# The second MoE's w_in products by Strassen's scheme, in spans of 768 tokens

## The chip, the cores and the metric

The kernel runs on one core of a Trainium2 chip. The metric is the device time of one execution in microseconds. The core's engines are TensorE (matmuls into PSUM), VectorE, ScalarE, GpSimd and SyncE, which issues all DMAs of this kernel; each works off its own instructions in the written order.

## What is computed

Retention attention over 8 batches, 8 heads, 576 positions and 64 dimensions, then two MoE layers over the 4608 tokens of width 512:

```python
x = attn_out.transpose(0, 2, 1, 3).reshape(4608, 512)
x = np.maximum(np.maximum(x @ w1, x @ w2), x @ w3) @ w_out   # first MoE, d_ff 768
h = x @ w_in                                                 # second MoE, d_ff 2048
g = h * np.clip(h + 3.0, 0.0, 6.0) / 6.0
out = g @ w_out
```

The weights come in as 64-bit floats and are turned into 32-bit ones on the chip. Every operand of a large matmul is split into a rounded high part and the rest (fp32r), and a product of two is three matmuls: high by high, high by rest, rest by high (`product`, L378).

## The kernel before, in words

The tokens are worked in nine blocks of 512 (TT = 9, TB = 512). Attention of block t + 1 is mixed into the first MoE of block t. `up` (L388) makes one product of the first MoE, 4 k-tiles by 3 matmuls of 512 columns; its result is copied by ScalarE (L397) or joined by VectorE (L399) and then split (`split`, L50: ScalarE rounds, VectorE subtracts). `down` (L404) sums the six hidden blocks into four PSUM tiles `o0` to `o3`; at the last one the four parts are split into `y` and stored to DRAM as `x2d`, high part and rest. Beside this, one step of `background` after every fourth block unpacks the second MoE's 32 weight tiles (`Weights.step`: VectorE, ScalarE and GpSimd) and stores them as `wbd`. In the last two token blocks they are read back into SBUF, where they then stay.

The second MoE loops over nine token blocks and, inside, 16 hidden blocks of 128 (the loop behind `drain`, L609). `hidden` (L560) is 12 matmuls of 512 columns: the weights are the stationary operand, the tokens stream. `gated` (L567) has VectorE form min(max(h + 3, 0), 6) h in two operations out of PSUM (L570, L571), ScalarE round it (L52), VectorE subtract (L53). `project` (L577) is 12 matmuls of 512 columns as well: the gated hidden block is stationary, w_out streams, and four 128-token rows of the output gather in `o0` to `o3` over all 16 hidden blocks. It runs two hidden blocks behind, so the gating has cover. `store` (L593) scales the four tiles (L600 VectorE, L603 ScalarE) into one of three `ob` tiles and issues their DMAs (L605). The next token block's `x` is loaded at the fifth hidden block.

The order of all engines is the order in which the instructions are written (a manual schedule). What `split` leaves for VectorE, and stores, are put on a list `late` and written out at the next `flush`. A tile from a pool waits until the readers of what was in its place are done. In PSUM two tiles `mm` take turns (L560's products), four are `o0` to `o3`, and two more are used by attention and free after it.

Of the kernel before, what the change touches and what calls it, by code (L numbers as in the profile page):

```python
# [16 lines left out]
P = 128  # L17
# [3 lines left out]
C = 64  # L21
# [5 lines left out]
TT = NT // TB  # L27
NA = 4 * F1
# [8 lines left out]
def retention_moe_moe2(ctx: ExitStack, tc, hi, lo, w_a, w_b, mask, qdec, kdec, grow, out):  # L37
# [17 lines left out]
    stage = ctx.enter_context(tc.tile_pool(name="stage", bufs=2))  # L55
    w_pool = ctx.enter_context(tc.tile_pool(name="w", bufs=NA))
    x_pool = ctx.enter_context(tc.tile_pool(name="x", bufs=2))
    dram = ctx.enter_context(tc.tile_pool(name="dram", bufs=1, space=bass.MemoryType.DRAM))
    x2_d = [dram.tile([P, 2, KM, TB], F32, name=f"x2d{t}") for t in range(TT)]
    xe_d = dram.tile([P, 2, KM, TB], F32, name="xed")  # L60
    wb_d = [dram.tile([P, 2, 512], F32, name=f"wbd{i}") for i in range(2 * F2)]
# [21 lines left out]
    class Weights:  # L83


        def __init__(self, src, order, sink):
            self.src, self.order, self.sink, self.work, self.w = src, order, sink, {}, {}
            self.fetched = self.steps = 0
# [8 lines left out]
        def step(self):  # L97

            n, self.steps = self.steps, self.steps + 1
            if 1 < n <= len(self.order) + 1:  # L100
                i = self.order[n - 2]
                w = self.sink(i)
                nc.scalar.copy(w[:, 0, :], self.work[i][3])
            if n < self.fetched:
# [4 lines left out]
                frac = stage.tile([P, 512], U32, tag="wf", bufs=3, name="wf")  # L109
# [17 lines left out]
            if 1 < n <= len(self.order) + 1:  # L127
                frac = self.work.pop(i)[3]
                nc.gpsimd.tensor_tensor(out=w[:, 1, :], in0=frac, in1=f32(w[:, 0, :]), op=ALU.subtract)
                self.w[i] = w  # L130

        def __getitem__(self, i):
            return self.w[i]

    def keep(i):
        return w_pool.tile([P, 2, 512], F32R, tag="w", name="w")

    def pair():
        return moe.tile([P, 2, 512], F32R, tag="hy", bufs=8, name="y")
# [5 lines left out]
    order_b = [u for f in range(F2) for u in (f, F2 + f)]  # L145
    wa = Weights(w_a, order_a, keep)
    wb_part = Weights(w_b, order_b, lambda i: pair())
# [240 lines left out]
    def up(t, f, j):  # L388
        x = xs[t]
        ps = ps_mm.tile([P, 512], F32, tag="mm", name="mm")  # L390
        for kk in range(KM):
            product(ps, wa[3 * f + j], slice(kk * P, (kk + 1) * P),
                    (x[:, 0, kk, :], x[:, 1, kk, :]), kk == 0, kk == KM - 1)
        flush()
        if j == 0:
            tmp[t, f] = moe.tile([P, TB], F32, tag="t", bufs=2, name="t")
            nc.scalar.copy(tmp[t, f], ps)  # L397
            return
        nc.vector.tensor_tensor(out=tmp[t, f], in0=ps, in1=tmp[t, f], op=ALU.max)  # L399
        if j == 2:  # L400
            h = hid[t, f] = moe.tile([P, 2, TB], F32R, tag="hy", bufs=8, name="h")
            split(tmp.pop((t, f)), h[:, 0, :], h[:, 1, :])

    def down(t, f):  # L404
# [5 lines left out]
        for m in range(KM):  # L410
            product(acc[t][m], wa[3 * F1 + f], slice(m * P, (m + 1) * P),
                    (h[:, 0, :], h[:, 1, :]), f == 0, f == F1 - 1)
            if f == F1 - 1:
                flush()
                y = pair()
                split(acc[t][m], y[:, 0, :], y[:, 1, :])
                late.append(lambda m=m, y=y: nc.sync.dma_start(out=x2_d[t][:, :, m, :], in_=f32(y)))
# [9 lines left out]

    x2, wb = {}, {}

    def load_x2(t):  # L430
        if t < TT:
            x2[t] = x_tile()
            nc.sync.dma_start(out=f32(x2[t]), in_=x2_d[t])

    with tc.manual_schedule():
# [52 lines left out]
        for n, blk in enumerate(blocks(0) + [lambda: down(0, F1 - 1)]):  # L488
# [7 lines left out]
            if n == 21:  # L496
                wb_part.fetch(2)
# [5 lines left out]
        def load_w(i, pool):  # L503
            wb[i] = pool.tile([P, 2, 512], F32R, tag="w", name="w")
            nc.sync.dma_start(out=f32(wb[i]), in_=wb_d[i])

        def background():

            if wb_part.steps >= len(order_b) + 2:
                return  # L510
            if not wb_part.fetched:
                wb_part.fetch(2)
            wb_part.step()
            for i in wb_part.w:
                if i not in wb:
                    wb[i] = None
                    late.append(lambda i=i: nc.sync.dma_start(out=wb_d[i], in_=f32(wb_part.w[i])))

        for t in range(1, TT):
# [9 lines left out]
            for n, blk in enumerate(todo):  # L529
# [5 lines left out]
                if t == B - 1:  # L535
                    if n == 2:
                        xs[B] = x_tile()
                        nc.sync.dma_start(out=f32(xs[B]), in_=xe_d)
                    if n >= 4 and n % 2 and n < 20:
                        load_w(order_b[n // 2 - 2], wx_pool)  # L540
                if t == B:
                    if n == 4:
                        load_x2(0)
                    if n < count - 3:
                        load_w(order_b[8 + n], w_pool)
            while side:
                side.pop(0)()
            if t == B - 2:
                flush()
                while wb_part.steps < len(order_b) + 2:  # L550
                    background()
                flush()
                at.release()
                ps_at.release()
                wx_pool = ctx.enter_context(tc.tile_pool(name="wx", bufs=8, side="right", reuse_waits="tile"))


        m2 = None

        def hidden(t, f):  # L560
            xh, xl = x2[t][:, 0], x2[t][:, 1]
            ps = ps_mm.tile([P, TB], F32, tag="mm", name="mm")
            for kk in range(KM):
                product(ps, wb[f], slice(kk * P, (kk + 1) * P), (xh[:, kk, :], xl[:, kk, :]), kk == 0, kk == KM - 1)
            return ps

        def gated(ps):  # L567
            flush()
            g = m2.tile([P, TB], F32, tag="g", bufs=2, name="g")
            nc.vector.tensor_scalar(out=g, in0=ps, scalar1=3.0, scalar2=0.0, op0=ALU.add, op1=ALU.max)  # L570
            nc.vector.scalar_tensor_tensor(out=g, in0=g, scalar=6.0, in1=ps, op0=ALU.min, op1=ALU.mult)  # L571
            gh = m2.tile([P, TB], F32R, tag="gh", bufs=3, name="gh")
            gl = m2.tile([P, TB], F32R, tag="gl", bufs=3, name="gl")
            split(g, gh, gl)
            return gh, gl

        def project(acc, w, g, f):  # L577
            flush()
            gh, gl = g
            for s in range(TB // P):  # L580
                c = slice(s * P, (s + 1) * P)
                nc.tensor.matmul(acc[s], lhsT=gh[:, c], rhs=w[:, 0, :], start=(f == 0), stop=False)  # L582
                nc.tensor.matmul(acc[s], lhsT=gh[:, c], rhs=w[:, 1, :], start=False, stop=False)  # L583
                nc.tensor.matmul(acc[s], lhsT=gl[:, c], rhs=w[:, 0, :], start=False, stop=(f == F2 - 1))  # L584

        def rows(t, s, c):

            if t < B:
                r0 = t * S + s * P
                return [(slice(0, P), out[r0:r0 + P, c])]  # L590
            return [(slice(C * i, C * (i + 1)), out[(2 * s + i) * S + TB:(2 * s + i + 1) * S, c]) for i in range(2)]

        def store(t, acc):  # L593
            for s in range(TB // P):
                ob = m2.tile([P, DM], F32, tag="ob", bufs=3, name="ob")
                parts = 2 if t == TT - 1 and s == TB // P - 1 else 1
# [92 lines left out]
```

## Time and profile before

| | us |
|---|---|
| median of 3 runs | 1570.11 |
| lowest and highest run | 1566.72, 1570.18 |
| the profiled execution | 1565.97 |
| its span, first to last instruction | 1564.1 |
| TensorE busy in it | 1515.7 (97%) |
| VectorE busy | 787.7 (50%) |
| ScalarE busy | 330.3 (21%) |
| GpSimd busy | 155.2 (10%) |

Sums from rows are made against the span of 1564.1 and the profiled execution's 1565.97, which lies 4.1 us under the median. Times in rows count from the first instruction. A matmul's record is longer than its distance from the next, since matmuls overlap: the distance between starts is what a matmul costs. Start and duration are in us, means by line in ns.

### The profile page before, as it was taken

The page shows a single profiled execution, that of the slowest core. Times are in us where ns is not written, and L with a number is a line of the kernel's source. Part 1 is how long each engine was busy: PE and PEld are TensorE (multiplying, and loading weights), DVE is VectorE, ACT ScalarE, POOL GpSimd, SP SyncE. Part 2 cuts the span into 40 slices and gives each one's busy share as a digit, 9 for nine tenths or more (in the row PEclk, how much of TensorE's full clock was granted, in tenths as well). Part 3 has the DMA queues.
Part 4 walks back from the last instruction along what each step waited for, and adds up shares of the span by engine and source line. Part 5 has one row for each costly group of instructions (what it writes and reads, how often), then busy time and mean ns, then how long its engine had stood idle before and what let it go on. Part 6 is the DMA issues. An engine that isn't in the chain of part 4 may idle for free.

```text
span 1564.1 us, 22512 instructions
## 1 busy us (share of the span) xinstructions
PE 1515.7 (97%) x9376; PEld 1229.8 (79%) x9376; DVE 787.7 (50%) x1669; ACT 330.3 (21%) x601; POOL 155.2 (10%) x180
## 2 busy tenths in 40 slices
PE   7689989999999999999999999999999999999998
PEld 4567768888888888888788888888888888888886
DVE  3997577777767776222333434343433334343432
ACT  3444223232323232111111111111111111111111
POOL 1345112212121211000000000000000000000000
PEclk9889999999999999999999999999999999999999
DMA  8564165656565653517600202020200202020001
GB/s 204 147 169 133 70 161 183 171 170 173 169 171 170 175 167 91 215 37 286 215 1 1 81 0 81 0 81 1 81 1 1 81 0 81 0 81 1 27 0 27
DMA packets 48582, 152.73 MB, mean 98 GB/s; under 512 B 13217, under 2 KB 13729, under 8 KB 43233
## 3 DMA queue, kind: packets, MB, share of 16 engines
q1 hardware_dynamic: 48480, 151.31, 32.0%
q8 instruction: 73, 1.20, 0.3%
q14 instruction: 29, 0.23, 0.0%
HBM read 104.10 MB, written 47.19 MB: 97 GB/s over the span
## 4 chain that ended last, share of the span: by engine, by line
PE 89%; DVE 5%; DMA 3%; issue 1%; POOL 1%; ACT 0%; SPq 0%; POOLq 0%; DVEq 0%; ACTq 0%
PE mm L382 18%; PE mm L384 17%; PE mm L383 17%; PE o L584 8%; PE o L582 8%; PE o L583 8%; PE o L382 3%; PE o L383 3%; PE o L384 3%; PE at L254 2%; PE at L212 2%; DMA raw<-in_lo 1%; DMA room<-in_lo 1%; DVE raw L247 1%; DVE raw L233 1%
## 5 line engine op out<-in xcount | busy, mean ns | idle before, releaser
L382 PE MATMUL mm<-x,w 128*128 128x512 f32 x1224 | 487.3, 398 | 3.5 <-ACT t L397 3.1
L383 PE MATMUL mm<-x,w 128*128 128x512 f32 x1224 | 480.1, 392 | 0.0
L384 PE MATMUL mm<-x,w 128*128 128x512 f32 x1224 | 480.1, 392 | 0.0
L382 PEld LDWEIGHTS mm<-x,w 128*128 128x128 f32 x1224 | 231.4, 189 | 56.4 <-ACT t L397 3.9
L570 DVE TENSOR_SCALAR g<-mm 128x512 f32<-128x512 f32 x144 | 99.5, 691 | 346.0 <-PE mm L384 345.8
L384 PEld LDWEIGHTS mm<-x,w 128*128 128x128 f32 x1224 | 231.2, 189 | 50.7
L383 PEld LDWEIGHTS mm<-x,w 128*128 128x128 f32 x1224 | 231.5, 189 | 47.6
L52 ACT CAST gh<-g 128x512 fp32r<-128x512 f32 x144 | 89.4, 621 | 688.7 <-DVE g L571 688.7
L584 PE MATMUL o<-w,gl 128*128 128x512 f32 x576 | 225.6, 392 | 3.6 <-DVE gl L53 3.6
L582 PE MATMUL o<-w,gh 128*128 128x512 f32 x576 | 225.7, 392 | 0.0
L583 PE MATMUL o<-w,gh 128*128 128x512 f32 x576 | 225.3, 391 | 0.0
L53 DVE TENSOR_TENSOR gl<-g,gh 128x512 fp32r<-128x512 f32 x144 | 99.6, 692 | 115.6 <-ACT gh L52 109.1
L399 DVE TENSOR_TENSOR t<-mm,t 128x512 f32<-128x512 f32 x108 | 74.3, 688 | 153.0 <-PE mm L384 151.8
L584 PEld LDWEIGHTS o<-w,gl 128*128 128x128 f32 x576 | 108.5, 188 | 27.5 <-DVE gl L53 4.1
L583 PEld LDWEIGHTS o<-w,gh 128*128 128x128 f32 x576 | 108.6, 189 | 23.4
L582 PEld LDWEIGHTS o<-w,gh 128*128 128x128 f32 x576 | 108.5, 188 | 23.3
L125 POOL TENSOR_TENSOR wf<-wf,wp 128x512 f32<-128x512 f32 x56 | 74.6, 1332 | 369.8 <-DVE wp L123 365.0
L571 DVE SCALAR_TENSOR_TENSOR g<-g,mm 128x512 f32<-128x512 f32 x144 | 99.0, 688 | 4.9
L247 DVE SCALAR_TENSOR_TENSOR raw<-raw,at 64x64 f32<-64x64 f32 x392 | 85.8, 219 | 11.3
L382 PE MATMUL o<-h,w 128*128 128x512 f32 x216 | 85.2, 394 | 0.0
L383 PE MATMUL o<-h,w 128*128 128x512 f32 x216 | 84.1, 390 | 0.0
L233 DVE TENSOR_TENSOR raw<-at,mask_sb 64x64 f32<-64x64 f32 (+2 forms) x172 | 61.6, 358 | 44.7 <-PE at L212 28.0
(76 smaller groups left out, 1132.6 us busy)
## 6 DMA issues: line engine op xcount, KB each, us to landing
x2d<-y SPq DMA_DIRECT2D x36, 512.0 KB, 3.9
x<-x2d SPq DMA_DIRECT2D x9, 2048.0 KB, 8.0
ws<-in_w_b SPq DMA_DIRECT2D x32, 512.0 KB, 7.8
wbd<-y SPq DMA_DIRECT2D x32, 512.0 KB, 3.0
w<-wbd SPq DMA_DIRECT2D x32, 512.0 KB, 6.4
raw<-in_hi SPq DMA_DIRECT2D x29, 560.0 KB, 5.6
raw<-in_lo SPq DMA_DIRECT2D x29, 560.0 KB, 7.8
ws<-in_w_a SPq DMA_DIRECT2D x24, 512.0 KB, 4.1
```

What stands on the lines that cost most here:

```text
L52: nc.scalar.copy(hi, full)
L53: late.append(lambda: (eng or nc.vector).tensor_tensor(out=lo, in0=full, in1=f32(hi), op=ALU.subtract))
L233: nc.vector.tensor_tensor(out=t[own, c0:c0 + n * C].rearrange("p (c s) -> p c s", s=C), in0=ps[other, p0:p0 + n * C].rearrange("p (c s) -> ...
L247: nc.vector.scalar_tensor_tensor(out=new, in0=old, scalar=gamma[2 * self.hp + e] ** C, in1=add, op0=ALU.mult, op1=ALU.add)
L382: nc.tensor.matmul(ps, lhsT=wh, rhs=xh, start=first, stop=False)
L383: nc.tensor.matmul(ps, lhsT=wh, rhs=xl, start=False, stop=False)
L384: nc.tensor.matmul(ps, lhsT=wl, rhs=xh, start=False, stop=last)
L570: nc.vector.tensor_scalar(out=g, in0=ps, scalar1=3.0, scalar2=0.0, op0=ALU.add, op1=ALU.max)
L571: nc.vector.scalar_tensor_tensor(out=g, in0=g, scalar=6.0, in1=ps, op0=ALU.min, op1=ALU.mult)
L582: nc.tensor.matmul(acc[s], lhsT=gh[:, c], rhs=w[:, 0, :], start=(f == 0), stop=False)
L583: nc.tensor.matmul(acc[s], lhsT=gh[:, c], rhs=w[:, 1, :], start=False, stop=False)
L584: nc.tensor.matmul(acc[s], lhsT=gl[:, c], rhs=w[:, 0, :], start=False, stop=(f == F2 - 1))
```

## The change

The product with w_in is made by Strassen's scheme (in Winograd's form): a span of 768 tokens is cut in two halves of 384, the 512 inputs in two halves of two k-tiles, and a pair of hidden blocks in its two blocks of 128. Seven products (`times`, 2 k-tiles by 3 matmuls of 384 columns) take the place of eight. There are 6 spans (p) and 8 pairs (j).

The seven weight operands of each pair are formed once by VectorE beside the first MoE (`form`, four operations of 128x256 per pair), stored to DRAM as `wqd`, and read back for every span and pair, 7 tiles of 256 KB each, one pair ahead (`load_wq`). The seven operands of the tokens are formed per span (`operand`: T1 to T4 by one VectorE difference each over 2 x 384 columns, then each of the seven is split); those of span p + 1 at j = 4 and 5 of span p (the first four), at j = 7 (T3, T4) and at j = 0 of their own span (B22). `x2d` holds the plain sum now, not high part and rest, and each span is read from it at j = 1 of the span before.

Two PSUM tiles X and Y gather partial sums in place: ScalarE copies X after the first, third and fifth product (`kept`), VectorE adds these to Y (`added`) or takes X itself, and `gated` works on 384 columns, out of SBUF for C11, C22 and C12. The projection with w_out has as many matmuls as before; its jobs are of one 128-token row and one hidden block (3 matmuls of 512 columns), six PSUM tiles instead of four, and two jobs follow each of six products (`project(2)`), working off the pair before. w_out stays in SBUF and is loaded in the last token block of the first MoE, into tiles that the first MoE's weights leave. The diff's core:

```diff
+    def w_tile():
+        return w_pool.tile([P, 2, 512], F32R, tag="w", bufs=F2, name="w")
+    def v_tile():
+        return w_pool.tile([P, 2, 512], F32R, tag="v", bufs=NA - F2, name="v")
...
+    def keep(i, full):
+        w = wa_sb[i] = w_tile() if len(wa_sb) < F2 else v_tile()
+        return [(w[:, 0, :], w[:, 1, :], full)]
...
+    def form(i, full):
+        if i >= F2:
+            w = pair()
+            late.append(lambda: nc.sync.dma_start(out=wo_d[i - F2], in_=f32(w)))
+            return [(w[:, 0, :], w[:, 1, :], full)]
+        j, one = i // 2, full.rearrange("p (q c) -> p q c", c=2 * P)
+        if i % 2 == 0:
+            first[j] = one
+            sums, at_ = [one], [0]
+        else:
+            old = first.pop(j)
+            two = moe.tile([P, TB], F32, tag="t", bufs=3, name="s").rearrange("p (q c) -> p q c", c=2 * P)
+            def put(out, a, b, op):
+                nc.vector.tensor_tensor(out=out, in0=a, in1=b, op=op)
+            put(two[:, 1], one[:, 0], one[:, 1], ALU.add)
+            put(two[:, 0], two[:, 1], old[:, 0], ALU.subtract)
+            put(one[:, 0], old[:, 0], one[:, 0], ALU.subtract)
+            put(old[:, 1], old[:, 1], two[:, 0], ALU.subtract)
+            sums, at_ = [two, one, old[:, 1:]], [2, 4, 6]
+        res = []
+        for full, q in zip(sums, at_):
+            n = full.shape[1]
+            w = quads(pair())[:, :n]
+            late.append(lambda w=w, q=q, n=n: nc.sync.dma_start(out=wq_d[j][:, q:q + n], in_=f32(w)))
+            res.append((w[:, :, 0, :], w[:, :, 1, :], full))
+        return res
...
+        def load_wq(p, j, q=None):
+            if q is None:
...
+            t = (m2 if j % 2 else xq_pool).tile([P, 2, 2 * P], F32R, tag=f"w{q}", name=f"wq{q}")
+            nc.sync.dma_start(out=f32(t), in_=wq_d[j][:, q])
+            wq.setdefault((p, j), {})[q] = t
...
+            if name == "T2":
+                v["T1"] = put(v["B11"], v["B12"], v["B11"])
+                v["T2"] = put(v["X"], v["B22"], v["T1"])
+            elif name == "T3":
+                v["T3"] = put(v["B12"], v["B22"], v["B12"])
+            elif name == "T4":
+                v["T4"] = put(v["B21"], v["B21"], v["T2"])
+            pool = m2 if p % 2 and name in FRONT else xq_pool
+            q = xq[p, name] = pool.tile([P, 2, KM // 2, TH], F32R, tag=name, name=name)
+            split(v[name], q[:, 0], q[:, 1])
...
                 if t == B:
-                    if n == 4:
-                        load_x2(0)
-                    if n < count - 3:
-                        load_w(order_b[8 + n], w_pool)
+                    if n == 1:
+                        xv = load_x2(0, f32(x_tile()).rearrange("p a k n -> p (a k n)")[:, :KM * TS + TS])
+                        load_wq(0, 0)
+                    if 1 <= n <= F2:
+                        load_wo()
+                    if 8 <= n and n % 2 == 0 and names:
+                        operand(0, xv, names.pop(0))
...
+        def gated(full, s0, f):
+            g = m2.tile([P, TH], F32, tag="g", bufs=2, name="g")
+            nc.vector.tensor_scalar(out=g, in0=full, scalar1=3.0, scalar2=0.0, op0=ALU.add, op1=ALU.max)
+            nc.vector.scalar_tensor_tensor(out=g, in0=g, scalar=6.0, in1=full, op0=ALU.min, op1=ALU.mult)
+            parts = v_tile()[:, :, :TH]
+            split(g, parts[:, 0], parts[:, 1])
+            return [(s0 + s, parts[:, :, s * P:(s + 1) * P], f) for s in range(TH // P)]
+        def added(a, b):
+            c = m2.tile([P, TH], F32, tag="cc", bufs=2, name="cc")
+            nc.vector.tensor_tensor(out=c, in0=a, in1=b, op=ALU.add)
+            return c
+        def kept(ps):
+            c = m2.tile([P, TH], F32, tag="c", bufs=4, name="c")
+            nc.scalar.copy(c, ps)
+            return c
...
+        def project(n):
+            for _ in range(min(n, len(todo))):
+                flush()
+                p, (s, g, f), start, stop = todo.pop(0)
+                if start:
+                    outs[s] = (ps_acc.tile([P, 512], F32, tag=f"o{s}", name=f"o{s}") if s < 4 else
+                              ps_x.tile([P, 512], F32, tag=f"p{s}", name=f"p{s}"))
+                gh, gl = g[:, 0], g[:, 1]
+                nc.tensor.matmul(outs[s], lhsT=gh, rhs=wo[f][:, 0, :], start=start, stop=False)
+                nc.tensor.matmul(outs[s], lhsT=gh, rhs=wo[f][:, 1, :], start=False, stop=False)
+                nc.tensor.matmul(outs[s], lhsT=gl, rhs=wo[f][:, 0, :], start=False, stop=stop)
+                if stop:
+                    store(p, s, outs[s])
+        groups = [(p, j) for p in range(NS) for j in range(F2 // 2)]
+        outs = {}
+        for p, j in groups:
+            after = groups[groups.index((p, j)) + 1:][:1]
+            X, Y = (ps_mm.tile([P, 512], F32, tag="mm", name="mm")[:, :TH] for _ in range(2))
+            new = {}
+            def times(ps, q, name, first, last):
+                w, x = wq[p, j][q], xq[p, name]
+                for kk in range(KM // 2):
+                    product(ps, w, slice(kk * P, (kk + 1) * P), (x[:, 0, kk, :], x[:, 1, kk, :]),
+                            first and kk == 0, last and kk == KM // 2 - 1, read=True)
+                if after and after[0] != (0, 1):
+                    load_wq(*after[0], q)
+            times(X, 0, "B11", True, True)
+            if (p, j) == (0, 0):
+                times(Y, 1, "B21", True, True)
+                down(TT - 1, F1 - 1)
+                flush()
+                moe.release()
+                x_pool.release()
+                m2 = ctx.enter_context(tc.tile_pool(name="m2", bufs=1, reuse_waits="tile"))
+                load_wq(0, 1)
+            c1 = kept(X)
+            project(2)
+            if (p, j) != (0, 0):
+                times(Y, 1, "B21", True, True)
+            if j == 0 and p:
+                operand(p, xv, "B22")
+            elif j == 1 and p + 1 < NS:
+                xv = load_x2(p + 1, m2.tile([P, KM * TS + TS], F32, tag="xf", name="xf"))
+            elif 4 <= j < 6 and p + 1 < NS:
+                operand(p + 1, xv, FRONT[2 * j - 8])
+            flush()
+            new["C11"] = gated(added(Y, c1), 0, 2 * j)
+            project(2)
+            times(X, 2, "T2", False, True)
+            c2 = kept(X)
+            project(2)
+            times(Y, 3, "T1", True, True)
+            if 4 <= j < 6 and p + 1 < NS:
+                operand(p + 1, xv, FRONT[2 * j - 7])
+            project(2)
+            times(X, 4, "T3", False, True)
+            c3 = kept(X)
+            flush()
+            new["C22"] = gated(added(Y, c3), TH // P, 2 * j + 1)
+            project(2)
+            times(X, 5, "T4", False, True)
+            if j == F2 // 2 - 1 and p + 1 < NS:
+                operand(p + 1, xv, "T3")
+            flush()
+            new["C21"] = gated(X, 0, 2 * j + 1)
+            project(2)
+            times(Y, 6, "B22", False, True)
+            if j == F2 // 2 - 1 and p + 1 < NS:
+                operand(p + 1, xv, "T4")
+            flush()
+            new["C12"] = gated(added(Y, c2), TH // P, 2 * j)
+            for name in ("C11", "C22", "C21", "C12"):
+                for job in new[name]:
+                    todo.append((p, job, j == 0 and name in ("C11", "C22"),
+                                 j == F2 // 2 - 1 and name in ("C21", "C12")))
```

## Rows read from the trace of the kernel before

**Rows 1.** The page: its first line, and the shares of the chain of waits.

```profile
span 1564.1 us, 22512 instructions
...
PE 89%; DVE 5%; DMA 3%; issue 1%; POOL 1%; ACT 0%; SPq 0%; POOLq 0%; DVEq 0%; ACTq 0%
```

**Rows 2.** Busy times by stage; columns: stretch, busy per engine, TensorE clock, DMA share, GB/s.

```profile
758.55:1556.66 798.11, 794.47 (x3469) 651.88 (x3467) 311.53 (x453) 100.67 (x166) 0.00 (x0) 1.00 0.10 37
500.00:758.55 258.55, 258.55 (x1743) 211.48 (x1743) 117.86 (x291) 56.40 (x102) 25.61 (x29) 1.00 0.49 160
720.00:724.00 4.00, 4.00 (x19) 3.32 (x18) 1.30 (x2) 0.00 (x0) 0.00 (x0) 1.00 1.03 419
```

**Rows 3.** Timeline of TensorE, second MoE; columns: start, duration, line, out<-in, shape.

```profile
1000.18 0.39 PE L582 MATMUL o<-w,gh 128*128 128x512 f32 x1
...
1005.62 0.39 PE L582 MATMUL o<-w,gh 128*128 128x512 f32 x1
```

**Rows 4.** Timeline of TensorE at the change of MoE.

```profile
774.14 0.66 PE L584 MATMUL o<-w,gl 128*128 128x512 f32 x1 [3.64 <-DVE gl L53]
774.60 0.63 PE L582 MATMUL o<-w,gh 128*128 128x512 f32 x1
775.03 0.63 PE L583 MATMUL o<-w,gh 128*128 128x512 f32 x1
```

**Rows 5.** Timeline of TensorE at the start of another token block.

```profile
942.45 0.40 PE L382 MATMUL mm<-x,w 128*128 128x512 f32 x1
...
945.24 0.39 PE L582 MATMUL o<-w,gh 128*128 128x512 f32 x1
```

**Rows 6.** Weight loads by line and shape; columns: count, busy us, mean ns, idle before.

```profile
L382 PEld LDWEIGHTS mm<-x,w 128*128 128x128 f32 x1224 | 231.4, 189 | 56.4 <-ACT t L397 3.9 <-DVE t L399 0.6 <-DVE yr L258 0.4
...
L212 PEld LDWEIGHTS at<-raw 64*64 64x64 f32 x1044 | 37.4, 138 | 36.7 <-issue 15.2 <-DVE raw L233 8.6 <-DMA raw<-in_hi 6.1
```

**Rows 7.** VectorE and ScalarE by line and shape; columns as in rows 6.

```profile
L53 DVE TENSOR_TENSOR gl<-g,gh 128x512 fp32r<-128x512 f32 x144 | 99.6, 692 | 115.6 <-ACT gh L52 109.1 <-DMA x2d<-y 6.5
...
L52 ACT CAST gh<-g 128x512 fp32r<-128x512 f32 x144 | 89.4, 621 | 688.7 <-DVE g L571 688.7
...
L111 DVE TENSOR_SCALAR wf<-ws 128x512 uint32<-128x512 uint32 x56 | 23.5, 419 | 0.0
L258 DVE TENSOR_TENSOR yr<-at,qdec_sb 128x256 f32<-128x256 f32 x56 | 23.5, 419 | 4.2 <-PE at L254 3.3
...
L603 ACT ACTIVATE ob<-o 128x512 f32<-128x512 f32 x18 | 9.8, 592 | 4.7 <-PE o L584 4.7
...
L603 ACT ACTIVATE ob<-o 128x256 f32<-128x256 f32 x1 | 0.4, 383 | 2.3 <-DVE ob L600 2.3
```

**Rows 8.** Timeline of VectorE and ScalarE, one hidden block's gating.

```profile
1000.38 0.69 DVE L570 TENSOR_SCALAR g<-mm 128x512 f32<-128x512 f32 x1 [2.57 <-PE mm L384]
...
1001.11 0.69 DVE L571 SCALAR_TENSOR_TENSOR g<-g,mm 128x512 f32<-128x512 f32 x1
...
1001.90 0.62 ACT L52 CAST gh<-g 128x512 fp32r<-128x512 f32 x1 [4.82 <-DVE g L571]
...
1002.56 0.69 DVE L53 TENSOR_TENSOR gl<-g,gh 128x512 fp32r<-128x512 f32 x1 [0.76 <-ACT gh L52]
```

**Rows 9.** Busy times of three stretches with gaps in TensorE's work; columns as in rows 2.

```profile
119.70:130.00 10.30, 7.23 (x31) 5.31 (x31) 8.02 (x13) 5.70 (x10) 5.08 (x5) 1.00 0.46 156
223.70:226.90 3.20, 0.43 (x4) 0.04 (x2) 2.90 (x13) 0.58 (x1) 0.94 (x1) 1.00 0.90 287
228.20:231.60 3.40, 3.40 (x10) 2.62 (x9) 0.83 (x2) 0.62 (x2) 0.00 (x0) 0.50 0.83 175
```

**Rows 10.** Waits from 720 us on; columns: who, for whom, total us, times, longest.

```profile
DVE gl L53 <- DMA x2d<-y: 6.5, 1, 6.5
```

**Rows 11.** Timeline of the end of the kernel.

```profile
1555.44 6.30 SPq L605 DMA_DIRECT2D out<-ob  x10
...
1559.09 0.38 ACT L603 ACTIVATE ob<-o 128x256 f32<-128x256 f32 x1 [2.32 <-DVE ob L600]
```

More of the change, by code (lines that the diff above doesn't have):

```diff
@@ L101, in step @@
                 i = self.order[n - 2]
-                w = self.sink(i)
-                nc.scalar.copy(w[:, 0, :], self.work[i][3])
+                full = self.work.pop(i)[3]
+                parts = self.sink(i, full)
+                for hi, _, part in parts:
+                    nc.scalar.copy(hi, part)
             if n < self.fetched:
@@ L501, in retention_moe_moe2 @@
             ahead.pop(0)()
[L503 to L505 removed]
         def background():
[L509 to L517 removed]
+            if wb.steps < len(order_b) + 2:
+                wb.step()
@@ L553, in retention_moe_moe2 @@
                 at.release()
+                stage.release()
                 ps_at.release()
[L555 to L565, printed above, removed]
@@ L577, in project @@
[L577 to L586, printed above, removed]
+                xq_pool = ctx.enter_context(tc.tile_pool(name="xq", bufs=1, side="right", reuse_waits="tile"))
@@ L593, in store @@
[L593 to L596, printed above, removed]
-                for i in range(parts):
-                    c = slice(i * DM // parts, (i + 1) * DM // parts)
-                    if (s + i) % 2:
-                        nc.vector.tensor_scalar(
-                            out=ob[:, c], in0=acc[s][:, c], scalar1=1.0 / 6.0, scalar2=None, op0=ALU.mult)
-                    else:
-                        nc.scalar.mul(ob[:, c], acc[s][:, c], 1.0 / 6.0)
-                    for part, to in rows(t, s, c):
-                        nc.sync.dma_start(out=to, in_=ob[part, c])
@@ L633, in retention_moe_moe2, with store @@
-        drain(0)
+                return [(slice(0, P), out[r0:r0 + P, :])]
+            return [(slice(C * i, C * (i + 1)), out[(2 * s + i) * S + TB:(2 * s + i + 1) * S, :]) for i in range(2)]
+        def store(p, s, ps):
+            ob = f32(v_tile()).rearrange("p a n -> p (a n)")[:, :DM]
+            if s % 2:
+                nc.vector.tensor_scalar(out=ob, in0=ps, scalar1=1.0 / 6.0, scalar2=None, op0=ALU.mult)
+            else:
+                nc.scalar.mul(ob, ps, 1.0 / 6.0)
+            t, s = divmod(p * TS // P + s, TB // P)
+            for part, to in rows(t, s):
+                nc.sync.dma_start(out=to, in_=ob[part])
@@ L636 @@
+        project(len(todo))
 def kernel(**inputs):
```

145 lines of the change are left out of this document (69 added, 76 removed).

## The prediction

> **What bounds the kernel now.** I read the page first: the span, and under it the chain of waits, which is TensorE for 89% [rows 1]. Then the busy times by stage [rows 2]: of the 798.1 us from the first product of the second MoE (758.55) to its last (1556.66) TensorE is busy 794.5, VectorE 311.5, ScalarE 100.7, and the DMA moves 37 GB/s. So in the stage that the change rewrites, time is the number of matmuls times their spacing. The spacing stands in the timeline [rows 3]: 24 matmuls of 512 columns (12 of w_in, 12 of w_out) from 1000.18 to 1005.62, so 226.7 ns each. 512 columns at 2.4 GHz are 213.3, so 13.3 ns are lost per matmul. (A record's 0.39 us overlaps the next one's; busy time per line is not cost.)
>
> The stage holds 1728 matmuls of w_in, 1728 of w_out and 12 of the first MoE's last down-product: 3468 x 226.7 = 786.2 us. The other 11.9 are a stop at the change of MoE, 3.64 idle and some 2 of slow clock, 5.6 [rows 4], and stretches with a wider spacing, 12 matmuls in 2.79 us or 232.5 ns [rows 5], some 6 in all. They don't come from DMA: 419 GB/s leave 19 matmuls in 4 us, no fewer than at rest [rows 2].
>
> **The change, part by part. Fewer columns.** A span of 768 tokens and a pair of hidden blocks take 7 products of 2 x 3 matmuls of 384 columns: 6 spans x 8 pairs x 42 = 2016 matmuls for 1728. No matmul in the trace has this shape. If the lost 13.3 ns are a fixed cost, one takes 160 + 13.3 = 173.3 ns; if they are a share, 170. Below 170 nothing speaks for it. From above the weight load bounds it: a record of 128x128 takes 189 ns, but one of 64x64 takes 138 [rows 6], so 64 columns less save only about 50 ns; the load itself is about 100 ns, the rest is fixed and may overlap. I take 173.3, next to the measured spacing, and keep 170 and 189 as ends. 2016 x 173.3 = 349.4, w_out unchanged 1728 x 226.7 = 391.7, the down-product 2.7: 743.8 us, 54.3 under the 798.1. The Trainium skill ("TensorE: Matmul & The Clock Gate", Back-to-back issue gap) gives N/2.4 + 2.5 ns, by which it would be 162.5 and 215.8; the trace disagrees with the second by 11 ns, and by the rule the saving on w_in would be 45.3 us where I have 42.3.
>
> **Waits in an ordinary iteration.** An iteration is 7 products of 6 x 173.3 = 1.04 us, with six calls of project between them, 6 x 226.7 = 1.36 us each: 15.44 us. X and Y are the only two PSUM tiles, and VectorE and ScalarE work in the written order. The tight place is the end. After the fifth product (T3) ends, call it 0, TensorE has 1.36 + 1.04 + 1.36 + 1.04 = 4.80 us of work before the next iteration writes X. Until then: ScalarE copies X, VectorE forms C22 (add, scalar, product), ScalarE rounds it, VectorE subtracts, and only then come the two operations on C21 that free X. Durations at 384 columns from [rows 7]: VectorE two-operand 0.555 (between 0.419 at 256 and 0.692 at 512), ScalarE from PSUM 0.49 (0.383 and 0.592), its cast 0.52. Hand-offs from [rows 8] with [rows 3]: a record ends 0.165 after the next matmul could start, VectorE starts 0.04 later, ScalarE 0.10 after VectorE, VectorE 0.04 after ScalarE. The scalar operation now reads SBUF, and a TENSOR_SCALAR from SBUF takes 0.419 for 512 where two-operand forms take 0.692 [rows 7], so 0.35 here. This gives copy 0.69, add 1.28, scalar 1.67, product 2.27, cast 2.89, subtract 3.48, C21 4.04 and 4.63, X free at 4.7. It fits by 0.1 us. I cost it at nothing; one use of this chain that is 0.1 us longer than the room costs 4.3 us in all (43 iterations). The Trainium skill ("VectorE: DVE Perf Modes", Mode 2x_2P) says that one-source operations in SBUF run two elements a cycle and two-source ones never do; the trace agrees, 0.419 against 0.692. Without that the scalar would take 0.555 and X be free at 4.9.
>
> **Waits at the five span boundaries.** Here the same chain carries the next span's operands, 768 columns each: VectorE 0.965, ScalarE cast 0.83 by the same slopes. In j = 7 T3's difference, cast and rest stand ahead of C21: 3.48, 4.45, 5.38, 6.38, then C21 6.94 and 7.53, X free at 7.6 instead of 4.8: a wait of 2.8. Behind it are C21's cast and rest (8.15, 8.75), T4's three (9.71, 10.64, 11.65) and C12's add, which frees Y, at 12.2; TensorE wants Y at 7.6 + 1.04 + 1.36 = 10.0: another 2.25. In j = 0 a store of 0.69 lies in the chain (+0.6). In j = 5, counted from the iteration's start, VectorE is done with the last iteration's C12 at 3.7; T2's two differences, cast and rest (4.68, 5.68, 6.62, 7.62) stand ahead of C11's add, so Y is free at 8.2, where the fourth product wants it after three products and three calls, 7.2 (+1.0). Together 6.65 us, five times: 33.
>
> **Clock.** After the stop of 3.64 us TensorE's spacing goes to 0.43 for 3.4 us, 1.2 GHz [rows 4]. A stretch with a gap of 2.8 us (223.7 to 226.9) was followed by 3.4 us at 0.50; one with two gaps, 3.1 us together, was not [rows 9]. So a fall after the 2.8 us wait is likely. It slows the work ahead of the 2.25 us wait, which covers it in part: between 0 and 1.7 us, 3 in all for five.
>
> **First iteration.** project has nothing to do, so X and Y come round without cover: copy of X behind the four copies of the down-product 1.3, second copy 0.8, third 0.8, C21 1.9: 5 us. The stop of before, where VectorE's rest of g waits 6.5 us for a tile that the x2d store still reads [rows 10], goes: by the order of allocation the new pool's first tiles lie where the x tiles were, which are done with by then. Ends 2 and 9.
>
> **Spacing, tail, other stages.** Wide stretches: 0 to 15 us (232.5 over 226.7 on all of it), I take 6 as before. Tail: before, 7.4 us from the last matmul's end at 1556.66 to the end of the span, with ten issues in 6.30 us and the last two copies behind a wait for ob [rows 11]; after, nothing waits for ob and the last four tiles queue eight issues: 5.9, so 1.5 less (ends 0 and 3). In the first MoE 32 differences of 128x256 come to VectorE (32 x 0.419 = 13.4 us), and 36 rests of y at 512 go (36 x 0.692 = 24.9) [rows 7]; TensorE is busy throughout there and VectorE under half [rows 2]: 0, ends -3 and +5. The loads of 1.8 MB per 15.4 us are 119 GB/s, a whole iteration ahead, under the 419 seen: 0.
>
> Sum: 743.8 + 33 + 3 + 5 + 6 = 790.8, against 798.1: -7.3; tail -1.5: -8.8. The profiled execution is 1565.97, so 1557.2, a ratio of 0.9944; on the median of 1570.11 that is 1561.
>
> **The rivals.** (A) The boundary waits are hidden: then 36 us more come out, 1525. For: VectorE has over 40% of the stage idle. Against: the order is written out, nothing can overtake. (B) The end of the ordinary chain is 0.5 us longer than I sum it: 0.4 x 43 = 17, 1578, slower. It decides where C21's second operation frees X over 0.31 us past the room of 4.80: (8.8 + 4.7) / 43; beyond that the kernel is slower by more than 0.3%. For: the margin is 0.1. Against: every duration is from a row. (C) The weight load bounds a 384-column matmul: at 188 ns, 14.7 x 2016 = 29.6, less 2.5 of boundary waits, 1588. Against: the load's slope in [rows 6]. It turns the gain at 177.7. The Trainium skill ("Perfetto Trace Analysis", Identifying the Most-Contended Engine) would judge TensorE's headroom by the load's busy share; this is 82% of the stage now [rows 2] and by the same record length would pass 100% of a 384-column product, which is this rival. (D) The clock falls twice at each boundary, uncovered: 5 x 2 x 1.7 = 17 for the 3 assumed, 1575.
>
> **How the numbers follow.** Forecast 0.50 (own range 1548 to 1572), A 0.12, B 0.14, C 0.12, D 0.12. The range 1530 to 1588 leaves out most of A and half of C. A difference under 0.3% (4.7 us) can't be told from none. Faster: 0.38 of the forecast, A 0.12, and 0.05 of the others, 0.55; same 0.17; slower 0.28.
>
> **What would show it.** Right: in the profile after, matmuls of 384 columns 173 ns apart; X waiting for C21's product (2.8 us) once a span at j = 0, then Y for C12's add (2.2 us), five of each; VectorE near 60% of the stage. Wrong: spacing of 185 or more (C); a wait at every iteration's start (B); no waits of over 1 us (A).

## The result and the profile after

The changed kernel takes 1551.06 us (median; 1550.30 to 1555.35) where the kernel before took 1568.41 beside it: ratio 0.9896, 95% interval 0.9871 to 0.9921, so 1% faster. The profiled execution took 1551.59 us, 14.4 less than the 1565.97 of before. The forecast was 1561 in a range of 1530 to 1588, faster with a chance of 0.55: sign and range hold, the size was 10 us off. Of these 5.6 are the forecast of the profiled execution (1557.2); the rest is that I scaled it to the median of before, which lay 4 us over its profiled execution, while the two agree after.

The busy times by stage answer to [rows 2]; columns: stretch, its length, busy time of PE, PEld, DVE, ACT and POOL, TensorE clock, DMA share, GB/s.

```profile
0.00:757.03 757.03, 718.06 (x5908) 576.86 (x5909) 476.73 (x1226) 241.34 (x457) 172.59 (x196) 0.98 0.53 152
757.03:1543.25 786.22, 766.43 (x3757) 682.08 (x3755) 425.10 (x792) 199.91 (x393) 0.00 (x0) 0.99 0.44 133
1543.25:1549.80 6.55, 0.16 (x1) 0.00 (x0) 0.69 (x1) 0.17 (x1) 0.00 (x0) 0.77 0.70 160
```

The second MoE, first product to last, takes 786.2 us where it took 798.1: 11.9 less. The first MoE takes 1.5 less (757.03 for 758.55) and the tail 0.9 (6.55 for 7.44); together 14.3. The 1.5 can't be credited to the change: in the runs below, whose first MoE is the same as that of the changed kernel, it ends anywhere between 755.3 and 761.3 us. In the changed stage TensorE, nearly always busy before, now stands still for 19.8 us, and its clock is 0.99.

The page: first line and chain of waits, which answer to [rows 1].

```profile
span 1549.8 us, 24664 instructions
PE 81%; DVE 11%; ACT 3%; DMA 3%; issue 1%; SPq 0%; ACTq 0%; POOL 0%; POOLq 0%; DVEq 0%
```

TensorE's share of the chain falls from 89% to 81%: work that VectorE did beside TensorE now sets the time in places. Which places, the waits of TensorE from 757 us on tell; columns: who, for whom, us in total, times, longest.

```profile
PE mm L438 <- DVE g L662: 13.0, 8, 2.2
PE mm L438 <- DVE cc L669: 4.2, 6, 1.7
PE mm L438 <- ACT c L674: 1.8, 3, 1.1
```

L662 is the second operation on C21, which frees X; L669 the addition of C12 or C11, which frees Y. (These are idle times between records. A record lasts about 0.165 us beyond the next one's start, so the wait in the instruction's start is that much longer, and a wait under 0.165 us isn't in this view at all.)

One span boundary, first TensorE, then VectorE, in the timeline; columns: start, duration, engine, line, operation, [idle before and releaser].

```profile
1012.26 0.33 PE L440 MATMUL mm<-B,wq 128*128 128x384 f32 x1
1014.84 0.44 PE L438 MATMUL mm<-B,wq 128*128 128x384 f32 x1 [2.24 <-DVE g L662]
...
1017.15 0.40 PE L705 MATMUL o<-w,v 128*128 128x512 f32 x1
1019.22 0.44 PE L438 MATMUL mm<-B,wq 128*128 128x384 f32 x1 [1.68 <-DVE cc L669]
```

```profile
1010.44 0.56 DVE L56 TENSOR_TENSOR v<-g,v 128x384 fp32r<-128x384 f32 x1 [0.58 <-ACT v L55]
1010.92 0.95 DVE L597 TENSOR_TENSOR xf<-xf 128x768 f32<-128x768 f32 x1
1012.77 0.96 DVE L56 TENSOR_TENSOR T<-xf,T 128x768 fp32r<-128x768 f32 x1 [0.90 <-ACT T L55]
1013.64 0.55 DVE L661 TENSOR_SCALAR g<-mm 128x384 f32<-128x384 f32 x1
1014.23 0.55 DVE L662 SCALAR_TENSOR_TENSOR g<-g,mm 128x384 f32<-128x384 f32 x1
1015.36 0.56 DVE L56 TENSOR_TENSOR v<-g,v 128x384 fp32r<-128x384 f32 x1 [0.58 <-ACT v L55]
1015.84 0.95 DVE L597 TENSOR_TENSOR xf<-xf 128x768 f32<-128x768 f32 x1
1017.74 0.96 DVE L56 TENSOR_TENSOR T<-xf,T 128x768 fp32r<-128x768 f32 x1 [0.95 <-ACT T L55]
1018.62 0.55 DVE L669 TENSOR_TENSOR cc<-mm,c 128x384 f32<-128x384 f32 x1
```

This is the picture of the forecast: T3's difference and rest (1010.92 to 1013.73, with 0.90 of waiting for ScalarE's cast between) stand ahead of C21, and X waits; T4's stand ahead of C12, and Y waits.

### The profile page after: what moved, and what is told of

Same layout as the page of the kernel before. It is cut to its first block, busy times and chain, and to the rows that moved or that the text cites. A ratio compares the mean times of both kernels' runs of the same rounds, so it can differ in the third digit from the quotient of the medians.

```text
span 1549.8 us, 24664 instructions
## 1 busy us (share of the span) xinstructions
PE 1484.6 (96%) x9664; PEld 1258.9 (81%) x9664; DVE 902.5 (58%) x2019; ACT 441.4 (28%) x850; POOL 172.6 (11%) x196
## 4 chain that ended last, share of the span: by engine, by line
PE 81%; DVE 11%; ACT 3%; DMA 3%; issue 1%; SPq 0%; ACTq 0%; POOL 0%; POOLq 0%; DVEq 0%
PE mm L438 16%; PE mm L440 15%; PE mm L439 15%; PE o L704 5%; PE o L705 5%; PE o L703 5%; PE o L438 3%; PE o L439 3%; PE o L440 3%; PE p L704 2%; PE p L703 2%; PE p L705 2%; PE at L310 2%; PE at L268 2%; DVE g L662 1%
## 5 line engine op out<-in xcount | busy, mean ns | idle before, releaser
L55 ACT CAST v<-g 128x384 fp32r<-128x384 f32 x192 | 98.5, 513 | 370.0 <-DVE g L662 361.3
L669 DVE TENSOR_TENSOR cc<-mm,c 128x384 f32<-128x384 f32 x144 | 79.9, 555 | 201.9 <-ACT c L674 191.7
L438 PE MATMUL mm<-x,w 128*128 128x512 f32 x468 | 190.1, 406 | 3.4 <-ACT t L453 3.0
L439 PE MATMUL mm<-x,w 128*128 128x512 f32 x468 | 184.9, 395 | 0.0
L440 PE MATMUL mm<-x,w 128*128 128x512 f32 x468 | 184.5, 394 | 0.0
L56 DVE TENSOR_TENSOR v<-g,v 128x384 fp32r<-128x384 f32 x192 | 107.2, 559 | 112.3 <-ACT v L55 112.3
L704 PE MATMUL o<-w,v 128*128 128x512 f32 x384 | 152.3, 397 | 0.0
L705 PE MATMUL o<-w,v 128*128 128x512 f32 x384 | 152.0, 396 | 0.0
L703 PE MATMUL o<-w,v 128*128 128x512 f32 x384 | 151.7, 395 | 0.0
L438 PE MATMUL mm<-T,wq 128*128 128x384 f32 x384 | 130.6, 340 | 2.5 <-ACT c L674 1.8
L440 PE MATMUL mm<-T,wq 128*128 128x384 f32 x384 | 129.5, 337 | 0.0
L439 PE MATMUL mm<-T,wq 128*128 128x384 f32 x384 | 129.2, 337 | 0.0
L674 ACT COPY c<-mm 128x384 f32<-128x384 f32 x144 | 68.8, 478 | 178.7 <-PE mm L440 178.7
L438 PE MATMUL mm<-B,wq 128*128 128x384 f32 x288 | 99.5, 345 | 17.3 <-DVE g L662 13.0
L438 PEld LDWEIGHTS mm<-x,w 128*128 128x128 f32 x468 | 89.4, 191 | 25.0 <-ACT t L453 4.0
L440 PEld LDWEIGHTS mm<-x,w 128*128 128x128 f32 x468 | 89.4, 191 | 19.3
L439 PEld LDWEIGHTS mm<-x,w 128*128 128x128 f32 x468 | 89.6, 192 | 17.3
L440 PE MATMUL mm<-B,wq 128*128 128x384 f32 x288 | 97.8, 339 | 0.0
L439 PE MATMUL mm<-B,wq 128*128 128x384 f32 x288 | 97.6, 339 | 0.0
```

The costliest lines, as they stand in the source:

```text
L55: nc.scalar.copy(hi, full)
L56: late.append(lambda: (eng or nc.vector).tensor_tensor(out=lo, in0=full, in1=f32(hi), op=ALU.subtract))
L669: nc.vector.tensor_tensor(out=c, in0=a, in1=b, op=ALU.add)
L703: nc.tensor.matmul(outs[s], lhsT=gh, rhs=wo[f][:, 0, :], start=start, stop=False)
L704: nc.tensor.matmul(outs[s], lhsT=gh, rhs=wo[f][:, 1, :], start=False, stop=False)
L705: nc.tensor.matmul(outs[s], lhsT=gl, rhs=wo[f][:, 0, :], start=False, stop=stop)
```

## The experiments

The theory: the gain is set by 2016 matmuls at 173.3 ns, less waits for X and Y at the span boundaries, which come from operands that stand ahead of the freeing operations, and less a wide spacing of unknown cause. The rivals: a weight load that bounds the narrow matmul, DMA behind the wide spacing, an ordinary chain of VectorE that is the limit anyway.

**What a narrow matmul costs (e2_shapes).** The kernel before, with w_in's products cut in width, in three groups of token blocks.

```
+ for c0, c1 in ([(0, 512)], [(0, 256), (256, 512)], [(0, 384), (384, 512)])[t // 3]:
      for kk in range(KM):
-         product(ps, wb[f], ..., (xh[:, kk, :], xl[:, kk, :]), ...)
+         product(ps[:, c0:c1], wb[f], ..., (xh[:, kk, c0:c1], xl[:, kk, c0:c1]), ...)
```

> The kernel before with the w_in products cut by columns: token blocks 0 to 2 in matmuls of 512 columns as before, 3 to 5 in two of 256, 6 to 8 in one of 384 and one of 128. It measures the spacing by shape without Strassen. A fixed cost of 13.3 ns per matmul: 384 columns at 173.3 ns, 256 at 120.0, 128 at 66.7. A share of 6.25%: 170.0, 113.3, 56.7. The weight load as long as its record: about 188 for all three. The load's slope, 100 ns: 173.3, 120 and 100 for 128 columns. Time over the kernel before: 15 us by the fixed cost, near 0 by the share, about 35 with a bound of 100 ns for 128 columns, over 100 with 188.

Measured: 1604.75 us in a single run, 39 over the kernel before. TensorE in the timeline, at 256, at 128 and at 384 columns:

```profile
1152.67 0.28 PE L382 MATMUL mm<-x,w 128*128 128x256 f32 x1
1152.79 0.28 PE L383 MATMUL mm<-x,w 128*128 128x256 f32 x1
1152.91 0.28 PE L384 MATMUL mm<-x,w 128*128 128x256 f32 x1
...
1450.48 0.28 PE L384 MATMUL mm<-x,w 128*128 128x128 f32 x1
1450.59 0.27 PE L382 MATMUL mm<-x,w 128*128 128x128 f32 x1
1450.70 0.28 PE L383 MATMUL mm<-x,w 128*128 128x128 f32 x1
...
1453.73 0.33 PE L382 MATMUL mm<-x,w 128*128 128x384 f32 x1
1453.90 0.34 PE L383 MATMUL mm<-x,w 128*128 128x384 f32 x1
1454.07 0.34 PE L384 MATMUL mm<-x,w 128*128 128x384 f32 x1
```

The starts are 120, 111 and 173 ns apart. From 512 to 384 to 256 columns the loss stays 13.3 ns (226.7 - 213.3, 173.3 - 160, 120 - 106.7), a fixed cost. At 128 columns that rule would give 66.7; 111 is another bound. The nearest candidate is the weight load, whose own columns didn't change, but no run shows it. Its record of 189 ns [rows 6] is then no bound: 384 and even 256 columns come faster. Rival C falls. The extra time agrees: 576 matmuls more at 256 columns x 13.3 ns = 7.7, and 576 at 128, which bring 173.3 + 111 for 226.7, 57.6 x 576 = 33.2: 41, for 39 measured.

**Does DMA widen the spacing (e3_noreload).** The changed kernel, with 322 of the 336 loads of w_in's operands left out; the products then use the weights of other pairs.

```
+ if (0, j % 2) in wq and q in wq[0, j % 2]:
+     wq.setdefault((p, j), {})[q] = wq[0, j % 2][q]
+     return
```

> The changed kernel with the weight operands of the first two pairs used for all pairs, so that 322 of 336 loads of 256 KB are left out (the products are made from the wrong weights, the work of all engines but the DMA is the same). Theory (the wide spacing is not from the DMA): matmuls stay at 175.5 and 230.9 ns on average, the time within 3 us of the changed kernel, 1551. Rival (119 GB/s of weights written to SBUF widen the spacing): 173.3 and 226.7, 12 us less, 1539.

Measured: 1552.41 us (1549.83 to 1556.95), ratio 0.9916 (0.9896 to 0.9937), against 0.9896 with the loads. Busy times of the stage, columns as above:

```profile
756.00:1542.00 786.00, 764.54 (x3754) 680.46 (x3752) 425.05 (x793) 200.10 (x393) 0.00 (x0) 1.00 0.07 25
```

The DMA share falls from 0.44 to 0.07, the stage keeps its 786.2 us (755.3 to 1541.5), and the mean spacing of undisturbed matmuls stays at 175.5 ns (384 columns) and 230.9 (512). The streaming of 1.8 MB per iteration costs nothing, and isn't the cause.

**Does the change of width (e8_width).** The faster kernel e1_spread (below), with w_out's products cut to 384 columns.

```
+ n = DM if start else TH
- nc.tensor.matmul(outs[s], lhsT=gh, rhs=wo[f][:, 0, :], ...)
+ nc.tensor.matmul(outs[s][:, :n], lhsT=gh, rhs=wo[f][:, 0, :n], ...)
  (the other two with :TH)
```

> The kernel of e1_spread, with w_out's products cut to 384 of 512 columns, all but the first of each output tile (36 of 1728 stay at 512). The output is so incomplete. It asks where the wide spacing comes from (means of 175.5 ns for 384 columns and 230.9 for 512, over the 173.3 and 226.7 of undisturbed stretches, some 12 us of the stage). Theory: from the change between widths; with one width almost everywhere all matmuls of the stage come 173 to 174 ns apart on average. Rival: from the change of operands or of tile at the start of each run of products; then the mean stays at 175.5 or more. Time: 1692 x 53.4 ns = 90 us less, and the iteration is 0.32 us shorter per call of project, so that the chain to C21, which has 0.3 us of room and two calls beside it, makes TensorE wait some 0.35 us in each of 48 iterations, 17 us: 1531 - 90 + 17 = 1458, by the theory 1447, with some 10 us either way for waits; the spacing decides, not the time.

Measured: 1464.24 us in a single run. Timeline of TensorE, a run of w_out's products and the start of a run of w_in's:

```profile
1100.24 0.33 PE L706 MATMUL o<-w,v 128*128 128x384 f32 x1
1100.41 0.33 PE L707 MATMUL o<-w,v 128*128 128x384 f32 x1
1100.59 0.33 PE L708 MATMUL o<-w,v 128*128 128x384 f32 x1
1100.76 0.34 PE L438 MATMUL mm<-T,wq 128*128 128x384 f32 x1
1100.94 0.34 PE L439 MATMUL mm<-T,wq 128*128 128x384 f32 x1
1101.11 0.34 PE L440 MATMUL mm<-T,wq 128*128 128x384 f32 x1
```

Neither theory holds alone. Over all undisturbed matmuls of the stage w_out's lie 174.5 ns apart, 1.2 over the base (4.2 over it in e1_spread, at 512), but w_in's 175.4, 2.0 over it, hardly less than the 2.2 of e1_spread. So the change of width goes with some 3 ns x 1728 = 5 us of the 11.7 us of wide spacing. (That w_out's matmuls are also narrower here doesn't explain it: in the kernel before, all at 512, they lie 1.3 ns over the base, 1.9 in the first six of a run, and w_in's 2.3.) The cause of the other 6 us or so is open. w_in's part of them, 4.4 us, isn't a cost of the start of a run, as the rival had it: its first six matmuls of a run in the changed kernel and its second six, where two products follow each other, both lie 175.5 ns apart on average, and in e5_groups (below) the last three of its runs of eighteen still 175.7. Only w_out's long runs come back to the base: at the end of the changed kernel, where only w_out is left, the matmuls lie 226 to 227 ns apart from the sixth on. In the time, the waits for X (40 of them, 12.8 us) are the cost of shorter covers: each call of project is 0.32 us shorter, and the chain to C21 had 0.3 us of room. Five waits for Y, up to 1.4 us, add 6.8.

**How near the ordinary chain is to its limit (e4_extra).** The changed kernel, with one more VectorE operation per iteration (a 128x384 addition whose result nobody uses) ahead of C21.

```
+ ex = m2.tile([P, TH], F32, tag="ex", name="ex")
+ nc.vector.tensor_tensor(out=ex, in0=c3, in1=c3, op=ALU.add)
```

> The changed kernel with one VectorE operation more per iteration, an addition of 128x384 between the rest of C22 and C21, which nothing uses. Theory (VectorE's chain to C21 ends 0.3 us ahead of TensorE's need in an ordinary iteration): the 0.56 us are hidden for 0.3 and cost 0.25 in 42 iterations and all of 0.56 at the boundaries: 11 + 3 = 14 us, 1565. Rival (VectorE, busy 58%, is not the bound anywhere in an ordinary iteration): under 4 us.

Measured: 1569.42 us (1567.11 to 1571.96), ratio 1.0022 (1.0012 to 1.0032): 18 us lost, the whole gain. Busy times of the stage:

```profile
759.29:1563.05 803.76, 781.05 (x3757) 685.61 (x3755) 447.24 (x840) 199.60 (x393) 0.00 (x0) 0.99 0.41 130
```

48 operations, 22 us of VectorE (447.2 for 425.1), cost the stage 17.8 us, 804.0 for 786.2 measured to the same point (the window shown ends 0.2 us earlier, at the start of the last matmul). The timeline of an ordinary iteration, VectorE and then TensorE:

```profile
971.16 0.55 DVE L763 TENSOR_TENSOR ex<-c 128x384 f32<-128x384 f32 x1
971.62 0.55 DVE L661 TENSOR_SCALAR g<-mm 128x384 f32<-128x384 f32 x1
972.21 0.55 DVE L662 SCALAR_TENSOR_TENSOR g<-g,mm 128x384 f32<-128x384 f32 x1
...
972.46 0.34 PE L440 MATMUL mm<-B,wq 128*128 128x384 f32 x1
972.82 0.44 PE L438 MATMUL mm<-B,wq 128*128 128x384 f32 x1
```

The extra operation delays C21 by 0.46 us, and X's first matmul comes 0.36 us after its forerunner. In the changed kernel that distance is 173 to 175 ns in 36 of 48 iterations, j = 2 to 7 of every span; here it is so in none, and 260 to 362 in those 36. So of 0.46 us up to 0.19 shows: the room was about 0.3 us. The changed kernel's own trace agrees: in its ordinary iterations the second operation on C21 ends 4.5 us after T3's product, and TensorE wants X at 4.8 to 4.9. With the late second matmul after each wait (0.1 us, below) an iteration takes 0.28 us more; these late matmuls weren't in the 14 us expected. Rival B had its mechanism right: the kernel would be no faster with 0.5 us more in this chain.

**Are the operands the cause of the boundary waits (e1_spread).** The changed kernel, with the next span's operands spread out: the differences T3 and T4 in the two free places of j = 6, T3's split behind C12 in j = 7, T4's and B22's in the two places of j = 0. The same operations, none added.

```
  if j == 0 and p:
-     operand(p, xv, "B22")
+     operand(p, xv, "T4")
...
+ elif j == 6 and p + 1 < NS:
+     operand(p + 1, xv, "T3", True)      # second place: "T4", True
...
+ elif j == 0 and p:                      # second place
+     operand(p, xv, "B22")
...
- if j == F2 // 2 - 1 and p + 1 < NS:     # ahead of C21: "T3"; ahead of C12: "T4"
-     operand(p + 1, xv, "T3")
+ if j == F2 // 2 - 1 and p + 1 < NS:     # behind C12
+     operand(p + 1, xv, "T3")
```

(With the last argument True only the difference is formed.)

> The changed kernel with the operands of the next span spread out: the differences for T3 and T4 are taken in j = 6 already, T3 is split behind C12 instead of ahead of C21, T4 in the first place of j = 0 and B22 in the second. The same operations, none left out. Theory (the waits at the span boundaries come from VectorE's written order, operand work ahead of C21 and C12): the five waits of 2.4 us on X and the five on Y (5.4 us in all) go, and the three falls of the clock behind them; 17 to 21 us less than the changed kernel, about 1532. Rival (VectorE has too much to do at a boundary, in whatever order): the waits come back at Y's add of C11 in j = 0, and under 5 us are gained, about 1547.

Measured: 1531.03 us (1528.43 to 1533.19), ratio 0.9776 (0.9761 to 0.9791); a second time, beside e7_t1, 1531.45 (0.9770 to 0.9809). That is 20 us less than the change as it was (19 by the two ratios to the kernel before), and faster than both kernels. The stage (columns as above) and the waits of TensorE from 757 us on, in the second run:

```profile
757.18:1520.87 763.69, 759.08 (x3757) 679.21 (x3755) 424.43 (x792) 198.44 (x393) 0.00 (x0) 1.00 0.45 136
PE mm L438 <- DVE g L664: 1.9, 4, 1.4
PE mm L438 <- ACT c L676: 1.6, 2, 1.1
PE mm L438 <- DVE cc L671: 0.4, 2, 0.2
```

All waits of 2.2 and 1.7 us are gone, no clock fall is left in the stage, and to the same point as the 786.2 it takes 763.9 us, 22.3 less. Summed from the starts, waits, slow clock and late second matmuls fall from 30.8 to 8.4 us, which is all of it; the spacing of the other matmuls is unchanged (175.5 and 230.9). 

> The kernel of e1_spread once more, beside e7_t1 on the same chip, so that the two can be told apart to less than half a per cent: 1531 by all theories.

**The last waits (e7_t1).** e1_spread, with T1's difference formed in j = 4 instead of j = 5.

```
  operand(p + 1, xv, FRONT[2 * j - 7])
+ if j == 4:
+     operand(p + 1, xv, "T1", True)
```

> The kernel of e1_spread, with T1's difference (0.95 us of VectorE) moved from the iteration j = 5, where it stands ahead of C11's addition, to the second place of j = 4. Theory: the waits for Y of about 0.3 us that are left at j = 5 (five of them, 1.5 us) go, and nothing comes in their place: 1.5 us less than e1_spread, 1529.5 with 1531 for it. Rival: the added operation pushes C22 and C21 of j = 4 back by up to 0.95 us past their 0.3 us of room, and the waits come back there on X: 0 to 3 us slower than e1_spread, 1531 to 1534.

Measured: 1529.67 us (1527.03 to 1531.87), ratio 0.9774 (0.9756 to 0.9792). The medians are 1.8 us apart on the same chip, which the intervals don't separate; the trace does, within the stage: 761.68 us for 763.69, and the waits for Y at j = 5 are gone. (In the profiled executions the first MoE, the same in both, hides it: it ends at 759.8 here and at 757.2 in e1_spread's second run.)

```profile
759.83:1521.51 761.68, 757.80 (x3757) 679.66 (x3755) 423.56 (x792) 198.44 (x393) 0.00 (x0) 1.00 0.45 137
PE mm L438 <- DVE g L665: 1.9, 4, 1.4
PE mm L438 <- ACT c L677: 1.6, 2, 1.1
```

What is left is the first iteration, and 0.3 us for X behind each j = 0 but the first.

**Longer runs of products (e5_groups, e6_groups_t1).** e1_spread, with four calls of project as 4, 4, 2, 2 instead of six of 2, so that widths change less often; then the same with T1's difference in j = 4.

```
  c1 = kept(X)
- project(2)
...
- project(2)        # behind c2
+ project(4)
```

> The spread kernel (e1_spread) with the twelve projection jobs of an iteration in four calls of 4, 4, 2 and 2 instead of six of 2; the same matmuls, in fewer groups of one width. Theory (the wide spacing is paid at each change between 384 and 512 columns, some 25 ns over the first matmuls of a group of 512 and 13 of a group of 384): in a group of twelve the later matmuls come back to 226.7 ns, and two changes each way less per iteration save 2 x 38 ns x 48 = 3.6 us of the stage of 763.7 us, about 1527 in all. Rival (the spacing is wide everywhere in this stage, whatever the groups): 230.9 and 175.5 ns on average as before, the stage within 1 us of 763.7. A third: the longer runs without project between the products uncover a wait, and the stage is longer.

> As e5_groups, with the difference for T1 taken in j = 4 instead of j = 5, so that one of T2's two differences is out of the way of C11. Theory (the last wait at a boundary, 0.3 us on Y in j = 5, is this difference): the five waits of 0.3 us go, 1.5 us less than e5_groups. Rival (Y waits there for the copy by ScalarE): no difference.

Measured: 1549.86 (ratio 0.9902; 0.9885 to 0.9919) and 1549.17 (0.9899; 0.9881 to 0.9917): 19 us lost against e1_spread. The mean spacing of 512 columns went from 230.9 to only 230.2. What was lost shows in the timeline of e5_groups, TensorE and VectorE:

```profile
955.66 0.34 PE L439 MATMUL mm<-B,wq 128*128 128x384 f32 x1
955.84 0.34 PE L440 MATMUL mm<-B,wq 128*128 128x384 f32 x1
956.24 0.45 PE L438 MATMUL mm<-B,wq 128*128 128x384 f32 x1
...
955.63 0.55 DVE L671 TENSOR_TENSOR cc<-mm,c 128x384 f32<-128x384 f32 x1
```

B22, B11 and B21 now run without a call of project between them, so Y is wanted 1.05 us after its last product, before C12's addition has freed it: 0.40 us from start to start for 0.174, of which the idle times show 0.06. The trace of e5_groups has 56 waits of 0.15 to 0.30 us (13.0 in all), five waits for Y of 1.1 us at j = 1 (5.5), and a late second matmul behind each; with them its stage is 20.6 us longer than e1_spread's. Of the two medians nothing can be said on T1 (0.7 us apart); the stage is 3.1 us shorter in e6_groups_t1 (781.5 for 784.6), and e7_t1 above shows the same without the longer runs.

## Why the prediction was right or wrong

| Term, us | forecast | measured |
|---|---|---|
| matmuls at base spacing | 743.8 | 743.8 |
| wide spacing | 6 | 11.7 |
| first iteration | 5 | 4.3 |
| boundaries, with the clock | 36 | 26.5 |
| stage | 790.8 | 786.2 (sum 786.3) |
| first MoE; tail | 0; -1.5 | -1.5; -0.9 |

The stage came out 4.6 us under the forecast because two sizes were off in opposite directions, the boundaries by 9.5 us too much and the wide spacing by 5.7 too little. That they cancel in part is luck, and the 1.5 us of the first MoE are the spread between executions.

**The matmul** was right: 173 to 174 ns is the commonest distance at 384 columns, and e2_shapes shows the fixed 13.3 ns. The Trainium skill's N/2.4 + 2.5 ("TensorE: Matmul & The Clock Gate", Back-to-back issue gap), which the page gives for a single matmul in isolation, would be 162.5 ns; measured are 173.3 here, 120 at 256 columns for its 109. For a stream with a weight load per matmul, as here, the page says that the two together set the spacing; the forecast quoted the formula without this limit. The measurement decides.

**The wide spacing** was mis-sized: 2.2 ns x 2016 = 4.4 and 4.2 ns x 1728 = 7.3 us. I carried over what stood in the kernel before; but the changed kernel switches between widths 12 times in an iteration, and e8_width ties some 5 us to that; the rest, about what stood there before, stays unexplained. The bounds (0 to 15) held it.

**The boundary waits** were right in place, number and releaser, and too large in three terms. (1) X: 2.4 us for 2.8. X was free 7.3 us after T3's product, not 7.6, and TensorE, with its wider spacing, wanted it at 4.9, not 4.8. In the timeline above VectorE's next operation starts before a subtraction's record (L56) ends (1012.77 + 0.96 = 1013.73, the next at 1013.64), 0.08 to 0.09 each time and twice in the chain; the other 0.14 are hand-offs that I took a little long. (2) Y, with the clock. From the last matmul before X's wait to the first after Y's wait is 6.96 us at all five boundaries (1012.26 to 1019.22; 1273.76 to 1280.72), though the clock fell to half (0.53 on average over the stretch below) in three of them (884, 1277 and 1407 us) and not in two (1014, 1145). So the fall cost nothing: it slowed only what then waited for VectorE. Busy times of the stretch with a fall, columns as above:

```profile
1277.00:1280.50 3.50, 3.50 (x10) 2.42 (x8) 2.55 (x4) 0.83 (x1) 0.00 (x0) 0.53 0.00 0
```

At the boundary shown first, without a fall, TensorE stood idle 1.68 us before Y; here 0.20. I had priced X, Y and clock at 2.8 + 2.25 + 0.6 = 5.65; it is 6.96 less 2.57 of matmuls, 4.4. (3) Y at j = 5: 0.28 to 0.35 us for 1.0, since VectorE was done with the last iteration's C12 at 3.3 us, not 3.7, and the chain after it ran 0.17 faster; a store in j = 0 shows 0.3 at the next X for 0.6, since the room of the ordinary chain takes the other half.

**The ordinary chain** was right in what it said (no wait) and short in the room: 0.1 forecast, about 0.3 measured in e4_extra, for the same reason as (1). The durations were right: 0.56 for the two-operand forms at 384, 0.36 for the scalar from SBUF (the Trainium skill's "VectorE: DVE Perf Modes", Mode 2x_2P, which the forecast followed, agrees: 0.36 here against 0.55 from PSUM), 0.96 at 768, casts 0.51 and 0.83. VectorE is busy for 54% of the stage, where near 60 was forecast.

**The rivals.** A, hidden boundary waits at 1525, was wrong as a forecast of this kernel, since the order is written out; as a price it was nearly right: with the order rewritten, e7_t1 takes 1529.7. B's mechanism is real, its condition wasn't met. C falls with e2_shapes. D falls: the clock falls at most once in a boundary, and covered.

## What to carry to other kernels

When a change takes work off TensorE and gives it to VectorE, lay the order of VectorE beside the order in which TensorE wants its PSUM tiles back: here the same operations in other places of the written order were worth 22 us of the stage, where the change itself had brought 12. Price the chain that frees a PSUM tile to a tenth of a microsecond, since every iteration pays what it lacks. And a gap in the view of waits can be shorter than what a record overlaps: sums of starts show waits that the view doesn't.

## What the runs showed of the hardware

A matmul of 384 or 256 columns costs its columns at 2.4 GHz and 13.3 ns, as one of 512 does; one of 128 columns costs 111 ns. Where runs of 384 and of 512 columns take turns, w_out's matmuls lie 4.2 ns over that, most of it in the first matmuls of a run (232.7 ns for the first three and 227.1 for the last three of the twelves in e5_groups); without a change of width the excess was 1.2 to 1.3. w_in's is 2.0 to 2.3 in the kernel before, the changed one and e8_width, and doesn't go away along a run. After a wait, the first matmul's follower comes about 0.105 us late (1014.84 to 1015.12, 280 ns for 174), which the twenty boundary waits of the changed kernel make some 2 us. Of five waits of 2.4 us three were followed by some 3.4 us at 1.2 GHz and two weren't; in e4_extra, where the same wait is 0.47 us longer, all five were. What tells the three from the two stays open.
